# Down and output projections as one row on the tensor engine, output written as four rows

## The chip, the cores and the metric

The kernel runs on one core of a Trainium2 chip. The metric is device time in microseconds (us), the median of several executions. A profile gives the span of one execution, from its first to its last instruction; it is a little shorter than the time (2518.0 against 2519.67 for the profiled execution of the kernel before). A transfer has landed when the last of its DMA engines has raised its semaphore (a counter); the trace holds the time of every such count, called the records of the semaphores below. PE is the tensor engine, PEld its weight loads, DVE the vector engine, ACT the scalar engine, SP the engine that issues most DMAs.

## The reference, cut to what matters

One decode step: attention of one query over a cache of 65536 keys in 32 heads, a small gated feed-forward layer, and a gated sum of both.

```python
g = sigmoid((x * gate_w).sum(-1, keepdims=True))
# a: q = x @ wq; per head softmax(q k^T / sqrt(128)) v; heads joined (4096) @ wo   -> 512 numbers
# b: (silu(x @ w_gate) * (x @ w_up)) @ w_down                                      -> 512 numbers
return g * a + (1 - g) * b                                                      # bf16, (1, 1, 512)
```

The two caches are 1 GB together and are read once. Everything the change touches computes or stores the 512 output numbers.

Of the kernel before, what the change touches and what calls it, by code (L numbers as in the profile page):

```python
# [7 lines left out]
ACT = mybir.ActivationFunctionType  # L8
ALU = mybir.AluOpType
AXIS = mybir.AxisListType  # L10
P = 128
# [68 lines left out]
def kernel(  # L80
# [14 lines left out]
    nc = tc.nc  # L95
    bf16 = mybir.dt.bfloat16
    f32 = mybir.dt.float32

    _, H, Sk, Dh = A_k_cache.shape
    D = A_x.shape[2]  # L100
    F = B_w_gate.shape[1]
    KT = D // P
    FT = F // P
    OT = D // P
# [4 lines left out]
    scale = float(Dh) ** -0.5  # L109
# [7 lines left out]
    def sb(name, shape, dtype):  # L117
        return consts.tile(shape, dtype, name=name)
# [18 lines left out]
    O_sb = sb("O_sb", [VB, VB * Dh], f32)  # L137
    o_all = sb("o_all", [P, H], f32)
    oT = sb("oT", [P, H], bf16)
    gval = sb("gval", [P, 1], f32)  # L140
    ngval = sb("ngval", [P, 1], f32)
    hT = sb("hT", [P, FT], bf16)
# [2 lines left out]
    xg = sb("xg", [1, D], bf16)  # L145
    s_t = sb("s_t", [1, 1], f32)
    tot = sb("tot", [P, H], f32)
    rest = sb("rest", [P, OT], f32)
    o_row = sb("o_row", [H, Dh], bf16)
    M = sb("M", [P, H], bf16)  # L150
    o_last = sb("o_last", [P, 1], bf16)
    out_sb = sb("out_sb", [P, OT], bf16)

    S_ps = [psum.tile([P, HK, R], f32, name=f"S_ps{i}") for i in range(2)]
    O_ps = psum.tile([VB, VB * Dh], f32, name="O_ps")
    m_sp = psum.tile([P, 512], f32, name="m_sp")
    m_c = psum.tile([P, 512], f32, name="m_c")
    m_x = psum.tile([P, 512], f32, name="m_x")
# [7 lines left out]
    def op(engine, key, fn, reads=(), writes=(), sem=None):  # L166
        plan.add(engine, key, fn, list(reads), list(writes), sem)

    def units(s, a, b):

        w = UNIT * Dh
        return [(s, u) for u in range(a // w, -(-b // w))]

    def view(s, a, t, n):
        return slot[s][:, a : a + t * n].rearrange("p (t n) -> p t n", t=t)

    def dma(key, out_ap, in_ap, writes=(), reads=(), sem=None, engine="SP"):
        op(
            engine, key, lambda: emit[engine].dma_start(out=out_ap, in_=in_ap),
            reads=reads, writes=writes, sem=sem or key,  # L180
        )
# [11 lines left out]
    def take():  # L193
        s = turn[0] % SLOTS
        turn[0] += 1
        return s
# [27 lines left out]
    op("POOL", "ones_b", lambda: nc.gpsimd.memset(ones_b, 1.0), writes=["ones_b"])  # L224
    op("DVE", "ones", lambda: nc.vector.memset(ones, 1.0), writes=["ones"])
    op("DVE", "oT0", lambda: nc.vector.memset(oT, 0.0), writes=["oT"])
    op("DVE", "rowsum0", lambda: nc.vector.memset(rowsum, 0.0), writes=["rowsum"])

    def select(name, out_ap, in_ap, src, pattern, mul):
# [16 lines left out]
    def mms(key, out_ap, pairs, reads, writes, start=True, stop=True):  # L246


        def fn():
            for i, (a, b) in enumerate(pairs):  # L250
                ins = nc.tensor.matmul(  # L251
                    out_ap, lhsT=a, rhs=b,
                    start=start and i == 0, stop=stop and i == len(pairs) - 1,
                )
            return ins

        op("PE", key, fn, reads, writes)

    def group(key, parts, reads, writes):


        def fn():
            for out_ap, pairs in parts:
                for i, (a, b) in enumerate(pairs):
                    ins = nc.tensor.matmul(  # L265
                        out_ap, lhsT=a, rhs=b, start=(i == 0), stop=(i == len(pairs) - 1)
                    )
            return ins

        op("PE", key, fn, reads, writes)  # L270

    def act(key, out_ap, in_ap, func, reads, writes, **kw):
        op(
            "ACT", key, lambda: nc.scalar.activation(out=out_ap, in_=in_ap, func=func, **kw),  # L274
            reads, writes,
        )

    def dve(key, fn, reads, writes):
        op("DVE", key, fn, reads, writes)
# [36 lines left out]
    def block(n, j, m):  # L316

        s, h = where["k", n], n // CH
        qb = q_bc[h % 2]
        q_rep = bass.AP(tensor=qb.tensor, offset=qb.offset, ap=[list(qb.ap[0]), [0, m], [1, Dh]])  # L320
        w = view(s, 0, KPP, Dh)[:, j : j + m, :]
        names = units(s, j * Dh, (j + m) * Dh)
        dve(
            "products", lambda: nc.vector.tensor_tensor(out=w, in0=w, in1=q_rep, op=ALU.mult),  # L324
            names + [("q_bc", h % 2)], names,
        )
        r = ring["S"] % 2
        ring["S"] += 1
        B = 512 // R
        group(  # L330
            ("sums", s, j, m, r),
            [
                (
                    S_ps[r][:, b : b + B, :],
                    [(ident, w[:, b : b + B, i * R : (i + 1) * R]) for i in range(Dh // R)],
                )
                for b in range(0, m, B)
            ],
            names + ["ident"], [("S_ps", r)],
        )  # L340
        todo.append((n, j, m, r))

    def gather():
        n, j, m, r = todo.pop(0)
        b = ring["Sb"] % 2
        ring["Sb"] += 1
        dve(
            "gather",
            lambda: nc.vector.tensor_reduce(  # L349
                out=S_sb[b][:, :m], in_=S_ps[r][:, :m, :], axis=AXIS.X, op=ALU.add  # L350
            ),
            [("S_ps", r)], [("S_sb", b)],
        )
        col = n * RS + j // EK
        act(
            "exp", P_sb[n % 2][:, j : j + m], S_sb[b][:, :m], ACT.Exp,
            [("S_sb", b), "rowsum"], [("P_sb", n % 2, u) for u in range(j // EK, (j + m) // EK)]
            + [("rowsum", col)],
            scale=scale, accum_out=rowsum[:, col : col + 1],
        )  # L360
# [25 lines left out]
    def diagonal():  # L386

        h = pending.pop(0)
        mms(
            ("diagonal", h == H - 1), m_c[:, 0:1],  # L390
            [(O_sb[:, j * Dh : (j + 1) * Dh], pick[:, j : j + 1]) for j in range(VB)],
            ["O_sb", "pick"], ["m_c"], stop=(h < H - 1),
        )
        if h < H - 1:
            act("o_all", o_all[:, h : h + 1], m_c[:, 0:1], ACT.Copy, ["m_c"], [("o_all", h)])
# [45 lines left out]
            ["gval"], ["ngval"],  # L441
        )

    def rows(key, w_v, names, cols, cname, ks):

        group(
            key,
            [
                (
                    m_x[:, b : b + 1],  # L450
                    [(w_v[:, k, bass.ds(b, P, OT)], cols[:, k : k + 1]) for k in ks],
                )
                for b in range(OT)
            ],
            names + [cname], ["m_x"],
        )

    def norm(h0, h1):
        w = CH * RS
# [24 lines left out]
    def turn_outputs(part):  # L484

        if part == 0:
            mms("t_ps", m_sp[:H, :Dh], [(oT, ident)], ["oT", "ident"], ["m_sp"])
            act("o_row", o_row, m_sp[:H, :Dh], ACT.Copy, ["m_sp"], ["o_row"])
        else:
            mms(  # L490
                "m_ps", m_sp[:, :H],
                [(sel[:, j, :], o_row[:, j * H : (j + 1) * H]) for j in range(RP)],
                ["sel", "o_row"], ["m_sp"],
            )
            act("M", M, m_sp[:, :H], ACT.Copy, ["m_sp"], ["M"])
# [5 lines left out]
    for n in range(N - 1):  # L501
        h, c = divmod(n, CH)
# [27 lines left out]
    n, h = N - 1, H - 1  # L530
    ws = take()
    WO = FT * D
    WL = WO + H * D
    wd, wo, wo_last = view(ws, 0, FT, D), view(ws, WO, H, D), view(ws, WL, 1, D)
# [3 lines left out]
    load("k", n, [EK] * (KPP // EK))  # L538
    load("v", n, V_END)
    turn_outputs(1)  # L540
    rows("b_ps", wd, units(ws, 0, WO), hT, "hT", range(FT))
    diagonal()
    for i, j in enumerate(range(0, KPP, EK)):
        block(n, j, EK)
        if i == 0:
            dve("rest", lambda: nc.vector.tensor_scalar_mul(rest, m_x[:, :OT], ngval),
                ["m_x", "ngval"], ["rest"])
            rows("a_ps", wo, units(ws, WO, WL), M, "M", range(H))
        if i == 2:
            dve(  # L550
                "rest2",
                lambda: nc.vector.scalar_tensor_tensor(
                    out=rest, in0=m_x[:, :OT], scalar=gval, in1=rest, op0=ALU.mult, op1=ALU.add
                ),
                ["m_x", "gval", "rest"], ["rest"],
            )
        while len(todo) > 1:
            gather()
    gather()
# [3 lines left out]
    for m in V_END:  # L563
# [7 lines left out]
        if at == 0:  # L571
            norm(h, H)
        at += m
    dve("o_last", lambda: nc.vector.tensor_scalar_mul(o_last, m_c[:, 0:1], tot[:, h:H]),
        ["m_c", ("tot", h)], ["o_last"])
    rows("l_ps", wo_last, units(ws, WL, WL + D), o_last, "o_last", [0])
    dve(
        "out_sb",
        lambda: nc.vector.scalar_tensor_tensor(
            out=out_sb, in0=m_x[:, :OT], scalar=gval, in1=rest, op0=ALU.mult, op1=ALU.add  # L580
        ),
        ["m_x", "gval", "rest"], ["out_sb"],
    )
    dma("out", out[0, 0].rearrange("(p b) -> p b", b=OT), out_sb, ["out"], ["out_sb"])
    op("SP", "end", None, reads=["out"])


# [74 lines left out]
```

## The kernel before: the parts that the change touches

The caches stream in blocks of 8 MB through three slots. Per block of K, DVE multiplies by the query in place, PE sums the products (the tiles `S_ps`), DVE gathers, ACT takes the exponential, and PE multiplies by V. The last block of keys is handled apart, in four pieces ("the tail" below, some 40 us). Into its PE work the two projections are mixed, in *column* form: every 128x128 block of a weight matrix is the stationary operand, and one column of 128 numbers moves. A result lies as 128 partitions x 4.

```python
def rows(key, w_v, names, cols, cname, ks):
    group(key,
        [(m_x[:, b : b + 1],
          [(w_v[:, k, bass.ds(b, P, OT)], cols[:, k : k + 1]) for k in ks])   # every 4th weight column
         for b in range(OT)],                                                 # OT = 4
        names + [cname], ["m_x"])
# ... the tail, in program order (PE keeps this order):
rows("b_ps", wd, ..., hT, "hT", range(FT))            # down projection, 4 x 14 matmuls
diagonal()
for i, j in enumerate(range(0, KPP, EK)):             # four pieces of the last K block
    block(n, j, EK)                                   # DVE products, PE sums
    if i == 0:
        # rest = (1 - g) * b
        rows("a_ps", wo, ..., M, "M", range(H))       # output projection of 31 heads, 4 x 32 matmuls
    if i == 2:
        # rest = g * a + rest
    while len(todo) > 1:
        gather()                                      # DVE gather, ACT exp, one piece behind
gather()
# last head: five groups of one-column matmuls into m_c, 128 + 64 + 32 + 16 + 16,
# each waiting for its piece of the last V block; the softmax sum after the first
# o_last = m_c / sum;  rows("l_ps", wo_last, ..., o_last, "o_last", [0]);  out_sb = g * m_x + rest
dma("out", out[0, 0].rearrange("(p b) -> p b", b=OT), out_sb, ...)   # 128 pieces of 8 bytes
```

The softmax here doesn't subtract the row's maximum and nothing guards it: scores larger than these inputs give would overflow.

## Time and profile before

Before the change: 2522.19 us median of 3 runs (2521.62 to 2523.8).

| what | before |
|---|---|
| span of the profiled execution | 2518.0 us |
| DMA, one queue | 99.8% of the span |
| PE / DVE / ACT busy | 78% / 50% / 4% |
| down projection, output projection on PE | 2.03 us, 4.41 us |
| output DMA, issue to landing | 2.9 us |

From the page of the kernel before (span; busy us, share and instructions of the engines; the main DMA queue with packets, MB and share; bytes read):

```profile
span 2518.0 us, 19423 instructions
...
PE 1975.5 (78%) x9115; PEld 821.6 (33%) x9115; DVE 1268.3 (50%) x290; ACT 98.0 (4%) x402; POOL 1.9 (0%) x9
...
q1 hardware_dynamic: 20880, 1087.78, 99.8%
...
HBM read 1087.77 MB, written 0.00 MB: 432 GB/s over the span
...
```

The loads set the time of everything up to the tail. The timeline of the tail (start, duration, engine, source line, operation, output<-inputs, shapes, count, idle time before and who ended it):

```profile
...
2479.12 2.03 PE L265 MATMUL m_x<-hT,slot_66 128*128 128x1 bf16 x56
...
2485.91 4.41 PE L265 MATMUL m_x<-M,slot_66 128*128 128x1 bf16 x128
...
2490.18 5.30 PE L265 MATMUL S_ps_102<-slot_67,ident 128*128 128x512 bf16 x16
...
2500.59 3.63 PE L265 MATMUL S_ps_102<-slot_67,ident 128*128 128x512 bf16 x16 [1.66 <-DVE slot_67 L324]
...
2504.06 3.35 PE L251 MATMUL m_c<-P_sb_84,slot_65 128*128 128x1 bf16 x128
...
2511.11 1.74 PE L251 MATMUL m_c<-P_sb_84,slot_65 128*128 128x1 bf16 x60 [1.23 <-issue]
...
2512.88 0.22 DVE L574 TENSOR_SCALAR o_last<-m_c,tot 128x1 bf16<-128x1 f32 x1 [4.85 <-PE m_c L251]
...
2513.55 0.22 DVE L579 SCALAR_TENSOR_TENSOR out_sb<-m_x,gval,rest 128x4 bf16<-128x4 f32 x1 [0.45 <-PE m_x L265]
2513.80 0.35 SPq L179 DMA_DIRECT2D out_dram<-out_sb  x1
```

First come the two projections (56 and 128 matmuls of one column into `m_x`), with score sums (`S_ps`) behind them, then a wait of 1.66 us for DVE, the last sums, and the last head (`m_c`), which follows the pieces of V as they land. The chain of work that ended last, in order of time:

```profile
...
2479.87 29.69 DMA slot_65<-in_A_v_cache_dram
...
2509.61 0.27 PE m_c L251 x4
2509.88 1.23 issue
2511.11 1.75 PE m_c L251 x60
...
```

The chain runs through a landing of V and then through PE, with 1.23 us in which PE did nothing that the profile can explain. The records of the semaphores put the landing of the last V piece at 2512.07 us, so the last 16 matmuls could not have started before that. The DMA view gives the output transfer (last column: us from issue to landing):

```profile
...
out_dram<-out_sb SPq DMA_DIRECT2D x1, 1.0 KB, 2.9
```

One view more matters: the granted clock of PE (the share of its full clock that it was given). Length of a stretch, busy time of PE, PEld, DVE, ACT, POOL in it, then the mean clock, the DMA share and GB/s:

```profile
...
2486.00:2490.00 4.00, 4.00 (x124) 4.00 (x123) 4.00 (x3) 0.35 (x2) 0.00 (x0) 1.00 1.03 442
2490.00:2494.00 4.00, 4.00 (x21) 1.64 (x19) 2.32 (x2) 0.00 (x0) 0.00 (x0) 0.60 1.07 455
...
```

Right behind the 128 one-column matmuls the clock fell to half (from 2490.82 to 2494.23 in the trace's record of the clock, hence the mean of 0.60), and 16 sums took 5.30 us instead of 3.63.

### The profile page before, as it was taken

What the parts mean: (1) busy time and instruction counts of PE and PEld (TensorE: products, weight loads), DVE (VectorE), ACT (ScalarE), POOL (GpSimd) and SP (SyncE); (2) the same over time, 40 slices, a digit from 0 to 9 for tenths busy, and PEclk for the clock granted to TensorE, in tenths of its full rate; (3) what the DMA queues carried; (4) which work ended last, traced back from release to release, by engine and by line L of the source; (5) the groups of instructions that cost most, each with busy time, mean ns of one, the idle gap of its engine ahead of it and who ended that gap; (6) DMA issues with size and microseconds to landing.
All of it is one profiled execution on the core that took longest, in us unless ns stands there. A gap on an engine that the chain in (4) does not pass through costs nothing.

```text
span 2518.0 us, 19423 instructions
## 1 busy us (share of the span) xinstructions
PE 1975.5 (78%) x9115; PEld 821.6 (33%) x9115; DVE 1268.3 (50%) x290; ACT 98.0 (4%) x402; POOL 1.9 (0%) x9
## 2 busy tenths in 40 slices
PE   4787877877778778778787787787877877878788
PEld 2233332333323333333333333333333332333334
DVE  3455364464553554645535546445455464464554
ACT  0000000000000000000000000000000000000000
POOL 0000000000000000000000000000000000000000
PEclk8888989989889889898898899898988989989898
DMA  9999999999999999999999999999999999999998
GB/s 423 431 432 432 434 434 437 433 433 433 433 436 434 435 433 436 434 433 433 434 435 436 433 433 433 434 434 434 435 434 436 433 433 433 433 435 436 435 433 369
DMA packets 20906, 1088.09 MB, mean 432 GB/s; under 512 B 2450, under 2 KB 2580, under 8 KB 2836
## 3 DMA queue, kind: packets, MB, share of 16 engines
q1 hardware_dynamic: 20880, 1087.78, 99.8%
q8 instruction: 16, 0.26, 0.0%
q14 instruction: 6, 0.05, 0.0%
q10 hardware_dynamic: 4, 0.00, 0.0%
HBM read 1087.77 MB, written 0.00 MB: 432 GB/s over the span
## 4 chain that ended last, share of the span: by engine, by line
DMA 46%; PE 39%; DVE 13%; ACT 1%; another core or an unknown queue 0%; issue 0%; SPq 0%; DVEq 0%
PE O_ps L251 18%; DMA slot_67<-in_A_k_cache_dram 16%; DMA slot_66<-in_A_k_cache_dram 15%; DMA slot_65<-in_A_k_cache_dram 14%; PE S_ps_101 L265 11%; PE S_ps_102 L265 9%; DVE slot_67 L324 4%; DVE slot_66 L324 4%; DVE slot_65 L324 3%; DVE S_sb_82 L349 2%; PE m_c L251 1%; DMA slot_65<-in_A_v_cache_dram 1%; ACT P_sb_83 L274 1%; PE m_x L265 0%
## 5 line engine op out<-in xcount | busy, mean ns | idle before, releaser
L265 PE MATMUL S_ps_101<-slot_65,ident 128*128 128x512 bf16 x672 | 196.5, 465 | 133.8 <-DVE slot_65 L324 133.8
L265 PE MATMUL S_ps_101<-slot_66,ident 128*128 128x512 bf16 x672 | 193.5, 459 | 133.5 <-DVE slot_66 L324 133.5
L265 PE MATMUL S_ps_101<-slot_67,ident 128*128 128x512 bf16 x704 | 195.2, 446 | 125.0 <-DVE slot_67 L324 125.0
L324 DVE TENSOR_TENSOR slot_67<-slot_67,q_bc_79 128x16384 bf16<-128x16384 bf16 (+1 forms) x28 | 208.2, 7469 | 144.0 <-DMA slot_67<-in_A_k_cache_dram 144.0
L349 DVE TENSOR_REDUCE S_sb_82<-S_ps_102 128x128 f32<-128x1024 f32 (+1 forms) x67 | 78.8, 1176 | 391.5 <-PE S_ps_102 L265 391.5
L324 DVE TENSOR_TENSOR slot_65<-slot_65,q_bc_78 128x16384 bf16<-128x16384 bf16 x22 | 190.2, 8688 | 148.1 <-DMA slot_65<-in_A_k_cache_dram 148.1
L324 DVE TENSOR_TENSOR slot_66<-slot_66,q_bc_78 128x16384 bf16<-128x16384 bf16 (+1 forms) x24 | 190.6, 7977 | 136.5 <-DMA slot_66<-in_A_k_cache_dram 120.9
L324 DVE TENSOR_TENSOR slot_66<-slot_66,q_bc_79 128x16384 bf16<-128x16384 bf16 x20 | 172.9, 8688 | 123.9 <-DMA slot_66<-in_A_k_cache_dram 123.9
L324 DVE TENSOR_TENSOR slot_65<-slot_65,q_bc_79 128x16384 bf16<-128x16384 bf16 x20 | 172.9, 8688 | 118.5 <-DMA slot_65<-in_A_k_cache_dram 118.5
L324 DVE TENSOR_TENSOR slot_67<-slot_67,q_bc_78 128x16384 bf16<-128x16384 bf16 x20 | 172.9, 8688 | 117.5 <-DMA slot_67<-in_A_k_cache_dram 117.5
L251 PE MATMUL O_ps<-slot_67,P_sb_83 128*4 128x512 bf16 x704 | 156.4, 383 | 28.8 <-ACT P_sb_83 L274 18.3
L251 PE MATMUL O_ps<-slot_65,P_sb_83 128*4 128x512 bf16 x704 | 153.7, 379 | 19.6 <-ACT P_sb_83 L274 19.6
L251 PE MATMUL O_ps<-slot_66,P_sb_84 128*4 128x512 bf16 x704 | 153.7, 379 | 19.3 <-ACT P_sb_84 L274 19.3
L265 PE MATMUL S_ps_102<-slot_67,ident 128*128 128x512 bf16 x704 | 157.7, 382 | 3.1 <-DVE slot_67 L324 3.0
L265 PEld LDWEIGHTS S_ps_101<-slot_65,ident 128*128 128x128 bf16 x672 | 75.9, 116 | 254.6 <-DVE slot_65 L324 144.4
L265 PEld LDWEIGHTS S_ps_101<-slot_66,ident 128*128 128x128 bf16 x672 | 75.0, 115 | 252.0 <-DVE slot_66 L324 144.3
L265 PEld LDWEIGHTS S_ps_101<-slot_67,ident 128*128 128x128 bf16 x704 | 76.8, 112 | 243.1 <-DVE slot_67 L324 136.1
L251 PE MATMUL O_ps<-slot_67,P_sb_84 128*4 128x512 bf16 x640 | 139.7, 379 | 18.3 <-ACT P_sb_84 L274 18.3
L251 PE MATMUL O_ps<-slot_65,P_sb_84 128*4 128x512 bf16 x640 | 139.7, 379 | 18.3 <-ACT P_sb_84 L274 18.3
L251 PE MATMUL O_ps<-slot_66,P_sb_83 128*4 128x512 bf16 x640 | 139.7, 379 | 17.5 <-ACT P_sb_83 L274 17.5
L265 PE MATMUL S_ps_102<-slot_66,ident 128*128 128x512 bf16 x672 | 148.8, 379 | 2.1 <-DVE slot_66 L324 2.1
L265 PE MATMUL S_ps_102<-slot_65,ident 128*128 128x512 bf16 x672 | 148.6, 379 | 0.2 <-DVE slot_65 L324 0.2
(83 smaller groups left out, 860.6 us busy)
## 6 DMA issues: line engine op xcount, KB each, us to landing
slot_66<-in_A_k_cache_dram SPq DMA_DIRECT2D x4, 2048.0 KB, 24.6
slot_67<-in_A_k_cache_dram SPq DMA_DIRECT2D x4, 2048.0 KB, 30.6
slot_65<-in_A_wq_dram SPq DMA_DIRECT2D x1, 4096.0 KB, 12.2
slot_66<-in_A_wo_dram SPq DMA_DIRECT2D x1, 4096.0 KB, 31.3
slot_65<-in_A_v_cache_dram SPq DMA_DIRECT2D x1, 4096.0 KB, 23.2
slot_65<-in_A_v_cache_dram SPq DMA_DIRECT2D x1, 2048.0 KB, 27.7
slot_65<-in_B_w_gate_dram SPq DMA_DIRECT2D x1, 1792.0 KB, 34.9
slot_65<-in_B_w_up_dram SPq DMA_DIRECT2D x1, 1792.0 KB, 38.6
```

The source lines that it names most:

```text
L251: ins = nc.tensor.matmul(out_ap, lhsT=a, rhs=b, start=start and i == 0, stop=stop and i == len(pairs) - 1,)
L265: ins = nc.tensor.matmul(out_ap, lhsT=a, rhs=b, start=(i == 0), stop=(i == len(pairs) - 1))
L274: "ACT", key, lambda: nc.scalar.activation(out=out_ap, in_=in_ap, func=func, **kw),
L324: "products", lambda: nc.vector.tensor_tensor(out=w, in0=w, in1=q_rep, op=ALU.mult),
L349: lambda: nc.vector.tensor_reduce(out=S_sb[b][:, :m], in_=S_ps[r][:, :m, :], axis=AXIS.X, op=ALU.add),
```

## The change

The intent: fewer, longer matmuls for the projections (the vector is the stationary operand with one column, 512 weights move), and an output that leaves in 4 pieces of 256 bytes instead of 128 of 8. The row lies on one partition, so eight float32 matmuls with one-row operands spread it over four partitions; the last head is added there with four-column weights `Z` that are zero except in one column.

```diff
-    rows("b_ps", wd, units(ws, 0, WO), hT, "hT", range(FT))
+    row("b_ps", wd, units(ws, 0, WO), hT, "hT", range(FT), m_x, "m_x")      # 14 matmuls of 512
+    act("row_b", row_b, m_x[0:1, :D], ACT.Copy, ..., scale=ngval[0:1, :])
     diagonal()
     for i, j in enumerate(range(0, KPP, EK)):
         block(n, j, EK)
         if i == 0:
-            rest = m_x * ngval                                  # DVE
-            rows("a_ps", wo, units(ws, WO, WL), M, "M", range(H))
+            row("a_ps", wo, units(ws, WO, WL), M, "M", range(H), m_sp, "m_sp")  # 32 of 512
+            act("row_a", row_a, m_sp[0:1, :D], ACT.Copy, ..., scale=gval[0:1, :])
         if i == 2:
-            rest = m_x * gval + rest                            # DVE
+            mms("rest_ps", m_sp[:OT, :P],
+                [(unit[:, OT * q : OT * (q + 1)], r[:, P * q : P * (q + 1)])
+                 for r in (row_b, row_a) for q in range(OT)], ...)
+            act("rest", rest, m_sp[:OT, :P], ACT.Copy, ...)
@@ ... the last head is summed into m_c as before
-    o_last = m_c * tot;  rows("l_ps", wo_last, ..., o_last, "o_last", [0])
+    Z[:, :: OT + 1] = m_c * tot                                 # 128 x 4, into a zeroed 128 x 16
+    mms("l_ps", m_x[:OT, :P],
+        [(Z[:, OT * q : OT * (q + 1)], wo_last[:, 0, P * q : P * (q + 1)]) for q in range(OT)], ...)
     out_sb = m_x * gval + rest
-    dma("out", out[0, 0].rearrange("(p b) -> p b", b=OT), out_sb, ...)
+    dma("out", out[0, 0].rearrange("(i p) -> i p", p=P), out_sb, ...)
```

(Cut: three memsets at the start, and the declarations. The assignments without a call stand for one instruction each.)

More of the change, by code (lines that the diff above doesn't have):

```diff
@@ L147 @@
     tot = sb("tot", [P, H], f32)
-    rest = sb("rest", [P, OT], f32)
+    row_a = O_sb[0:1, :D]
+    row_b = sb("row_b", [1, D], f32)
+    unit = sb("unit", [1, OT * OT], f32)
+    rest = sb("rest", [OT, P], f32)
+    Z = sb("Z", [P, OT * OT], bf16)
     o_row = sb("o_row", [H, Dh], bf16)
     M = sb("M", [P, H], bf16)
-    o_last = sb("o_last", [P, 1], bf16)
-    out_sb = sb("out_sb", [P, OT], bf16)
+    out_sb = sb("out_sb", [OT, P], bf16)
     S_ps = [psum.tile([P, HK, R], f32, name=f"S_ps{i}") for i in range(2)]
@@ L226 @@
     op("DVE", "oT0", lambda: nc.vector.memset(oT, 0.0), writes=["oT"])
+    op("DVE", "Z0", lambda: nc.vector.memset(Z, 0.0), writes=["Z"])
+    op("DVE", "unit0", lambda: nc.vector.memset(unit, 0.0), writes=["unit"])
+    op("DVE", "unit1", lambda: nc.vector.memset(unit[:, :: OT + 1], 1.0), writes=["unit"])
     op("DVE", "rowsum0", lambda: nc.vector.memset(rowsum, 0.0), writes=["rowsum"])
@@ L442, in gate, with row @@
         )
-    def rows(key, w_v, names, cols, cname, ks):
-        group(
-            key,
-            [
-                (
-                    m_x[:, b : b + 1],
-                    [(w_v[:, k, bass.ds(b, P, OT)], cols[:, k : k + 1]) for k in ks],
-                )
-                for b in range(OT)
-            ],
-            names + [cname], ["m_x"],
-        )
+    def row(key, w_v, names, cols, cname, ks, bank, bname):
+        mms(key, bank[0:1, :D], [(cols[:, k : k + 1], w_v[:, k, :]) for k in ks],
+            names + [cname], [bname])
     def norm(h0, h1):
@@ L540 @@
     turn_outputs(1)
-    rows("b_ps", wd, units(ws, 0, WO), hT, "hT", range(FT))
+    row("b_ps", wd, units(ws, 0, WO), hT, "hT", range(FT), m_x, "m_x")
+    act("row_b", row_b, m_x[0:1, :D], ACT.Copy, ["m_x", "ngval"], ["row_b"], scale=ngval[0:1, :])
     diagonal()
@@ L545 @@
         if i == 0:
-            dve("rest", lambda: nc.vector.tensor_scalar_mul(rest, m_x[:, :OT], ngval),
-                ["m_x", "ngval"], ["rest"])
-            rows("a_ps", wo, units(ws, WO, WL), M, "M", range(H))
+            row("a_ps", wo, units(ws, WO, WL), M, "M", range(H), m_sp, "m_sp")
+            act("row_a", row_a, m_sp[0:1, :D], ACT.Copy, ["m_sp", "gval"], ["O_sb"],
+                scale=gval[0:1, :])
         if i == 2:
-            dve(
-                "rest2",
-                lambda: nc.vector.scalar_tensor_tensor(
-                    out=rest, in0=m_x[:, :OT], scalar=gval, in1=rest, op0=ALU.mult, op1=ALU.add
-                ),
-                ["m_x", "gval", "rest"], ["rest"],
+            mms(
+                "rest_ps", m_sp[:OT, :P],
+                [
+                    (unit[:, OT * q : OT * (q + 1)], r[:, P * q : P * (q + 1)])
+                    for r in (row_b, row_a)
+                    for q in range(OT)
+                ],
+                ["unit", "O_sb", "row_b"], ["m_sp"],
             )
+            act("rest", rest, m_sp[:OT, :P], ACT.Copy, ["m_sp"], ["rest"])
         while len(todo) > 1:
@@ L573 @@
         at += m
-    dve("o_last", lambda: nc.vector.tensor_scalar_mul(o_last, m_c[:, 0:1], tot[:, h:H]),
-        ["m_c", ("tot", h)], ["o_last"])
-    rows("l_ps", wo_last, units(ws, WL, WL + D), o_last, "o_last", [0])
+    dve(
+        "Z",
+        lambda: nc.vector.tensor_scalar_mul(
+            Z[:, :: OT + 1], m_c[:, 0:1].to_broadcast([P, OT]), tot[:, h:H]
+        ),
+        ["m_c", ("tot", h)], ["Z"],
+    )
+    mms(
+        "l_ps", m_x[:OT, :P],
+        [(Z[:, OT * q : OT * (q + 1)], wo_last[:, 0, P * q : P * (q + 1)]) for q in range(OT)],
+        ["Z"] + units(ws, WL, WL + D), ["m_x"],
+    )
     dve(
@@ L579 @@
         lambda: nc.vector.scalar_tensor_tensor(
-            out=out_sb, in0=m_x[:, :OT], scalar=gval, in1=rest, op0=ALU.mult, op1=ALU.add
+            out=out_sb, in0=m_x[:OT, :P], scalar=gval[:OT, :], in1=rest,
+            op0=ALU.mult, op1=ALU.add,
         ),
@@ L583 @@
     )
-    dma("out", out[0, 0].rearrange("(p b) -> p b", b=OT), out_sb, ["out"], ["out_sb"])
+    dma("out", out[0, 0].rearrange("(i p) -> i p", p=P), out_sb, ["out"], ["out_sb"])
     op("SP", "end", None, reads=["out"])
```

## The prediction

> **What bounds the kernel.** The page shows the DMA queue busy for 99.8% of the span, 1088 MB at 432 GB/s; PE is busy 78%, DVE 50%, ACT 4%. The loads of the K and V caches set the time. The change touches neither them nor anything in the loop (three small memsets at the start fall into idle DVE time), so all of its effect lies in the last 40 us of 2518.
>
> **The tail before (timeline and chain of waits, last 80 us).** The chain ends: V landing, `m_c` matmuls (to 2512.86), `o_last` 0.22, four `m_x` matmuls 0.28, `out_sb` 0.22, output DMA issued at 2513.80, landed about 2.9 us later, span end 2518.0. The landings put the last V piece at 2512.07, so the end is set by DMA, but PE runs close behind: its order is down projection (56 one-column matmuls, 2.03 us), diagonal 1.05, score sums 3.63, output projection (128 one-column matmuls, 4.41), sums 5.30, sums 3.6, a wait of 1.66 for DVE, sums 3.63, then `m_c`.
>
> **Costs on PE.**
> - Down projection: 14 matmuls of 512 columns, at the 227 ns a piece of the sums (3.63 us for 16): 3.2 us, +1.1; 0.3 us of it hides in an existing wait.
> - Output projection: 32 such, 7.2 us, +2.8.
> - The sums behind it ran at granted clock 0.5 from about 2490.9 to 2494 after the run of one-column matmuls, 5.30 us instead of 3.63. The Trainium skill, "TensorE: Matmul & The Clock Gate", Part 1, says that an idle window of about 3.4 us halves the clock[...]. 512-column matmuls should keep it at 1.0: -1.7.
> - New float32 spread, 8 matmuls recorded as 16 (the `pick` matmuls: 8 records in 1.05 us): estimate 2.2 us, of which 1.66 fits the wait for DVE: +0.5.
> Together the last sums end about 2.2 us later (estimate 1.5 to 4). `m_c` now starts at about 2506.3 instead of 2504; its 256 matmuls plus the norm need about 7.3 us: 2513.5 against 2512.86. A gap of 1.23 us before, at 2509.9, absorbs most of the delay. So about +0.5 us reaches the end (0 to 2).
>
> **The end.** `Z`, 4 matmuls with four-column weights, `out_sb`: each within 0.1 us of what it replaces. The output goes as 4 rows of 256 B instead of 128 pieces of 8 B. The old completions spread from 2515.1 to 2516.7; [...] 1.8 us passed between the last packet and the last completion. Only the spread can shrink: -0.3 to -1.5, say -0.8.
>
> **Sum.** +0.5 - 0.8: nothing visible. Predicted 2522 us (2517.5 to 2526.5, which is mainly variation between chips and runs). Faster by over 2%: 0.005; within 2%: 0.985; slower by over 2%: 0.01.
>
> **What would show it right or wrong.** Timeline of the tail: output projection 7 us, the sums after it 3.6 us, clock 1.0 in windows from 2490 to 2500 us; last sums ending 1.5 to 4 us later; `m_c` ending within 2 us of the last V landing, not limited by it alone; output landing under 2.9 us after issue. The first 2470 us identical, 432 GB/s.
>
> **What would make it wrong.** The clock dropping during the 512-column run (427 ns each would add some 7 us); float32 matmuls with a moving row of 128 much slower than estimated; an instruction fetch falling into the PE tail; the row copies on ACT (1 partition, 512 elements) delaying the exponentials; a different DMA rate on the chip used.

PE was busy for 4.00 us of the 4 from 2486 to 2490.

## The result, and the profile after

The changed kernel took 2519.97 us median of 4 runs (2519.86 to 2522.85), the kernel before 2521.9 in 4 runs (2520.1 to 2523.8). The ratio is 0.9995, interval 0.9978 to 1.0012: no difference can be seen. The page after:

```profile
span 2518.2 us, 19173 instructions
...
PE 1980.7 (79%) x8993; PEld 820.1 (33%) x8993; DVE 1268.7 (50%) x291; ACT 99.2 (4%) x405; POOL 1.9 (0%) x9
...
q1 hardware_dynamic: 20744, 1087.78, 99.7%
...
```

PE has 122 matmuls fewer and is busy 5 us longer; the loads moved the same bytes. The tail of the changed kernel, the same lines as before:

```profile
...
2480.20 3.18 PE L258 MATMUL m_x<-slot_66,hT 128*1 128x512 bf16 x14
...
2487.85 7.07 PE L258 MATMUL m_sp<-slot_66,M 128*1 128x512 bf16 x32
...
2494.85 3.63 PE L272 MATMUL S_ps_104<-slot_67,ident 128*128 128x512 bf16 x16
...
2503.70 3.63 PE L272 MATMUL S_ps_104<-slot_67,ident 128*128 128x512 bf16 x16
...
2507.16 3.40 PE L258 MATMUL m_c<-P_sb_84,slot_65 128*128 128x1 bf16 x128
...
2510.86 3.55 PE L258 MATMUL m_c<-P_sb_84,slot_65 128*128 128x1 bf16 x128
...
2514.45 0.23 DVE L580 TENSOR_SCALAR Z<-m_c,tot 128x4 bf16<-128x4 f32 x1 [3.04 <-PE m_c L258]
...
2515.36 0.34 DVE L592 SCALAR_TENSOR_TENSOR out_sb<-m_x,gval,rest 4x128 bf16<-4x128 f32 x1 [0.68 <-PE m_x L258]
2515.72 0.34 SPq L182 DMA_DIRECT2D out_dram<-out_sb  x1
```

The output projection takes 7.07 us instead of 4.41, but the sums behind it take 3.63 instead of 5.30, because the clock stays up:

```profile
...
2490.00:2494.00 4.00, 4.00 (x20) 1.60 (x19) 2.99 (x1) 0.00 (x0) 0.00 (x0) 1.00 1.04 442
...
```

From the start of the down projection to the end of the last sums, the changed kernel needs 2503.70 + 3.63 - 2480.20 = 27.13 us, the kernel before 2500.59 + 3.63 - 2479.12 = 25.10. PE reaches the last head later, and its chain shows no landing of V in this stretch:

```profile
...
2501.93 1.83 PE m_sp L258 x16
2503.77 3.56 PE S_ps_104 L272 x16
2507.33 3.24 PE m_c L258 x128
...
2511.01 3.42 PE m_c L258 x128
...
```

The last V piece landed at 2512.18 us, but PE did not finish `m_c` before 2514.41. So the end was set by PE, and the output DMA went out at 2515.72, 1.92 us later than before. It then landed at 2516.90, 1.18 us after issue, against 2.87 before (both from the records of the semaphore; the DMA view gives no landing for the new form). 1.92 lost and 1.69 won back leave the 0.2 us between the spans of 2518.2 and 2518.0.

One caution belongs here. The tail of this execution already *started* 1.08 us later than that of before (2480.20 against 2479.12). That is not the change: the first sums of the block before, the same instructions in both kernels, ran at half clock in this execution (5.33 us in the chain, from 2443.93) and at full clock in the other (3.63 us). That slow stretch comes and goes with either kernel: it is there in the kernel before with nine outputs (below), and absent in the second run of the changed kernel. Traces of these kernels start their tail anywhere between 2479.0 and 2483.0 us. Below, stretches are therefore counted from the start of the down projection.

### The profile page after: what moved, and what is told of

Same layout as the page of the kernel before. It is cut to its first block, busy times and chain, and to the rows that moved or that the text cites. A ratio compares the mean times of both kernels' runs of the same rounds, so it can differ in the third digit from the quotient of the medians.

```text
span 2518.2 us, 19173 instructions
## 1 busy us (share of the span) xinstructions
PE 1980.7 (79%) x8993; PEld 820.1 (33%) x8993; DVE 1268.7 (50%) x291; ACT 99.2 (4%) x405; POOL 1.9 (0%) x9
## 4 chain that ended last, share of the span: by engine, by line
DMA 44%; PE 41%; DVE 13%; ACT 1%; another core or an unknown queue 0%; issue 0%; SPq 0%; DVEq 0%; ACTq 0%
PE O_ps L258 18%; DMA slot_67<-in_A_k_cache_dram 16%; DMA slot_66<-in_A_k_cache_dram 14%; DMA slot_65<-in_A_k_cache_dram 14%; PE S_ps_103 L272 12%; PE S_ps_104 L272 9%; DVE slot_67 L331 4%; DVE slot_66 L331 4%; DVE slot_65 L331 3%; DVE S_sb_82 L356 2%; PE m_c L258 1%; ACT P_sb_83 L281 1%; DMA slot_65<-in_A_wq_dram 0%; PE m_sp L258 0%; PE m_x L272 0%
```

## The experiments

Theory: PE work in the tail reaches the end of the changed kernel, and costs about 2 us; the output transfer is about 1.7 us shorter, because its pieces are larger; the two cancel. Rivals: the end is set by the loads and neither matters; or the old landing was slow only because loads had just ended; or the number of DMA engines that report, not the size of the pieces, makes the old landing slow.

### The output transfer, nine times in a row

The first four kernels ran on one chip, one execution each. The addition is

```diff
     dma("out", ...)
+    for _ in range(8):
+        dma("out", ..., ["out"], ["out_sb"])      # each waits for the one before it
```

to the kernel before (128 pieces of 8 bytes) and to the changed kernel (4 of 256):

> The kernel before, its output DMA (128 pieces of 8 B) issued nine times in a row, each after the one before it has landed. Theory: landing took 2.87 us from issue in the profile of before and stands on the end of the span, so eight more add 8 x about 2.95, some 24 us: span near 2542. Rival (the long landing of before came from the loads still in flight just before it, not from its form): the eight repeats run on an idle memory and take 1.2 to 1.5 us each, 10 to 12 us in all.

> The changed kernel, its output DMA (4 rows of 256 B) nine times in a row. Theory: 1.18 us each as in the profile of after, with the issue about 1.25: eight more add about 10 us, span near 2528. Rival: the form does not matter, then the same addition as in the run with 128 pieces.

In the third kernel the four rows of the changed kernel are written in pieces of 8 bytes (`out[0, 0].rearrange("(r q b) -> q r b", q=OT, b=OT)`; the result is permuted, wrong), in the fourth a zeroed tile of 16 rows of 64 bytes is written (also wrong):

> The changed kernel with its four rows written in pieces of 8 B (result permuted, wrong on purpose), nine times. If the size of the pieces makes the landing slow, about 2.9 us each (+24 us); if the number of DMA engines that must report does (16 before, 4 after), about 1.2 us each (+10 us).

> The changed kernel, but the output written from a zeroed tile of 16 rows of 64 B (wrong on purpose), nine times. If the size or the number of the pieces makes the landing slow, 64 B pieces land nearly as the rows of 256 B do, 1.2 to 1.5 us each (+10 to 12 us); if the number of DMA engines does, about 2.9 us (+24 us).

The timelines (SPq: start of the first issue, time to the end of the last) in that order: 128 pieces of 8 bytes,

```profile
...
2514.56 28.08 SPq L179 DMA_DIRECT2D out_dram<-out_sb  x9
```

4 rows of 256 bytes,

```profile
...
2518.15 9.56 SPq L182 DMA_DIRECT2D out_dram<-out_sb  x9
```

4 rows in pieces of 8 bytes,

```profile
...
2515.93 29.64 SPq L182 DMA_DIRECT2D out_dram<-out_sb  x9
```

16 rows of 64 bytes,

```profile
...
2515.69 10.84 SPq L183 DMA_DIRECT2D out_dram<-fake  x9
```

(The spans were 2547.3, 2529.9, 2550.1 and 2528.8 us.) The stretch contains eight full transfers and one last issue of 0.35 us. One transfer took (28.08 - 0.35) / 8 = 3.47 us with 128 pieces of 8 bytes, (9.56 - 0.35) / 8 = 1.15 with 4 of 256, (29.64 - 0.35) / 8 = 3.66 with 8 bytes from four partitions, and (10.84 - 0.35) / 8 = 1.31 with 16 of 64. The loads were over, so "the loads disturbed it" falls; the theory's own 2.95 per transfer with 8-byte pieces was somewhat low. The Trainium skill, "DMA: Bandwidth & Descriptors", section "Why a DMA increments its semaphore by 16 and not by 1", says how many DMA engines take part: 16 for a tile of 128 or 16 rows, 4 for 4 rows, with the issuing sequencer adding the missing increments at once. The trace agrees: a transfer of the kernel before leaves 16 increments, one of the changed kernel five, the first 0.46 us after issue and the others at 1.12 to 1.18. Sixteen engines with 64 bytes are fast and four engines with 8 bytes are slow, so the number of engines is not the cause; the pieces are. Size and number of the pieces change together in these runs: in both fast forms each engine carries one piece, in the slow ones 8 and 32 (128 pieces over 16 and over 4 engines). Which of these it is stays open.

### Does the output form alone account for its share?

In the changed kernel only the output DMA is altered: it writes 128 pieces of 8 bytes from a zeroed tile, still waiting for the result. Its output is wrong, which doesn't matter for the time. Five rounds.

> The changed kernel with nothing altered but the output DMA: 128 pieces of 8 B from a zeroed tile, waiting for the same result (wrong on purpose). Theory: the output lands 2.5 to 3.3 us after issue instead of 1.2, span 1.3 to 2.1 us longer than the changed kernel, 2519.3 to 2520. Rival (the output form is hidden): 2518.

```profile
...
2516.30 0.35 SPq L183 DMA_DIRECT2D out_dram<-fake  x1
```

```profile
...
out_dram<-fake SPq DMA_DIRECT2D x1, 1.0 KB, 2.9
```

The first fence is the end of its timeline, the second its DMA view. From the start of the down projection (2480.79) to the output issue it needs 35.51 us, the changed kernel 2515.72 - 2480.20 = 35.52: nothing else changed. The landing went from 1.18 to 2.89 us. The span was 2520.5 us, a little over the range, since this execution's tail had also started 0.6 us later. The median was 2522.19 us (2521.39 to 2523.96), ratio to before 1.0006 (0.9992 to 1.0020). The rival, an output form that is hidden, falls.

### One half of the change at a time

These ran together with the changed kernel on one chip, five rounds each; the kernel before had 2521.39 us median there (9 runs, 2519.78 to 2523.92).

> The changed kernel once more, as the reference of this set. Theory: the end is set by PE, m_c ends 1 to 2.5 us after the last V landing, output lands about 1.2 us after issue, span 2516.5 to 2518.5, median within 1.5 us of before.

It took 2520.07 us (2519.6 to 2521.24), ratio 0.9995 (0.9982 to 1.0009), span 2517.9. `m_c` ended at 2514.09, 2.0 us after the last V landing (2512.06), and the output landed 1.18 us after issue. From the start of the down projection to the end of the last sums: 27.12 us, the 27.13 of the first trace.

First the projections as rows, but turned back to 128x4 columns, with last head and output as before:

```diff
-    rows("b_ps", ...);  rows("a_ps", ...)
+    row("b_ps", ..., m_x, "m_x");  row("a_ps", ..., m_sp, "m_sp")     # as in the changed kernel
+    # at i == 2: m_sp[:, b] = sum over r of (row_b, row_a) of r[:, b::4] (weights) x [[1.0]]
     dma("out", out[0, 0].rearrange("(p b) -> p b", b=OT), out_sb, ...)
```

> Only the first half of the change: both projections as one row on PE, but then spread to 128x4 columns, last head and output DMA as before. Theory (PE work added in the tail reaches the end, and the output form pays it back): last sums end as late as after (about 27 us from the start of the down projection, against 25.1 before), output landing 2.9 us, span 1.5 to 2 us longer than after, about 2519.5. Rival (PE has slack in the tail and the end is set by the loads): m_c ends as before, span 2518.0.

It took 2524.83 us (2523.44 to 2525.76), ratio 1.0010 (0.9997 to 1.0024), with a span of 2524.0: 4.5 us worse than expected. The timeline:

```profile
...
2503.12 0.62 PE L267 MATMUL m_sp<-ones,row_b 1*128 1x1 f32 x2
...
2506.97 5.00 PE L267 MATMUL S_ps<-slot,ident 128*128 128x512 bf16 x16
...
```

This way of turning the row back was a bad tool. Eight float32 matmuls with 128-column weights took from 2503.12 to 2506.97, 3.85 us instead of the 1.83 of the spread in the changed kernel. They move one column each; while they ran, at 2506.37, the clock fell to half, and the last sums took 5.00 us instead of 3.63. Another 1.3 us is chance: this tail started at 2481.46, that of the changed kernel at 2480.20. The three (2.0, 1.4 and 1.3) about make up the 4.5. The run agrees with the theory in sign (more PE work before the last sums ends later), but it does not isolate the rows; the single-change run above does that for the output side.

Then the other half. The projections are columns, with each weight block contiguous, the sum is turned to four rows by one matmul, and last head and output are those of the changed kernel:

```diff
-    row("b_ps", ...);  row("a_ps", ...);  spread by `unit`
+    rows(...) with w_v[:, k, P * b : P * (b + 1)] as weights       # 56 and 128 one-column matmuls
+    mms("rest_ps", m_sp[:OT, :P], [(rest_c, ident_f)], ...)         # 128x4 -> 4x128, float32
```

> Only the second half: both projections as columns as before, the sum turned to four rows by one matmul, last head and output DMA as after. Theory: last sums 25.1 to 26 us from the start of the down projection, clock at 0.5 for about 3.4 us after the output projection, m_c ends less than 1 us after the last V landing, output lands in 1.2 us: span about 2516.3, 1.5 us under both kernels. Rival (the output form is worth nothing by itself): span 2518.

It took 2518.27 us in five runs (2518.27 to 2518.35), ratio 0.9986 (0.9973 to 1.0000), and is correct: the fastest kernel, and the steadiest. Its slowest run was faster than the fastest of the 9 runs of the kernel before (2519.78) and of the 5 of the changed kernel (2519.6) on this chip, so this gain of over 1 us shows in the times too. Timeline, then chain:

```profile
...
2486.08 3.35 PE L270 MATMUL m_x<-M,slot 128*128 128x1 bf16 x128
...
2514.09 0.35 SPq L181 DMA_DIRECT2D out_dram<-out_sb  x1
```

```profile
...
2481.86 30.27 DMA slot<-in_A_v_cache_dram
...
2512.18 0.60 PE m_c L256 x16
...
```

The chain (its DMA line ends at 2512.13) now goes straight from the landing of the last V piece to the last 16 matmuls and the end: PE had caught up and waited for every piece of V. The output landed at 2515.26, 1.17 us after issue; the span was 2516.6, 1.4 us under that of before and 1.6 under that of the changed kernel. Two lines of the expectation were missed: the clock stayed at 1.00 (mean of 2488 to 2492), and the last sums ended 2498.02 + 3.63 - 2480.15 = 21.50 us after the start of the down projection instead of 25.1 to 26. They would fit the 4.41 us of the strided weights.

This run differs from before in two things, the output form and the contiguous weights. So the second alone was put into the kernel before (result permuted, wrong), five rounds, on the chip of the run with only the output altered:

```diff
-    [(w_v[:, k, bass.ds(b, P, OT)], cols[:, k : k + 1]) for k in ks]
+    [(w_v[:, k, P * b : P * (b + 1)], cols[:, k : k + 1]) for k in ks]
```

> The kernel before with its column matmuls loading contiguous weight blocks instead of every fourth column (result permuted, wrong on purpose); this is the other thing in which the run with columns and a row output differs from before. Theory: the 128 projection matmuls take 3.35 us instead of 4.41 and the clock stays at 1.0 behind them, so PE reaches the last V pieces earlier and waits for them; the output still lands 2.9 us after issue: span 2517.5 to 2518, clearly over the 2516.6 of columns with row output. Rival (the faster columns were the gain, not the output): span about 2516.6.

```profile
...
2486.13 3.35 PE L265 MATMUL m_x<-M,slot 128*128 128x1 bf16 x128
...
2498.07 3.63 PE L265 MATMUL S_ps<-slot,ident 128*128 128x512 bf16 x16 [1.66 <-DVE slot L324]
...
2512.20 0.59 PE L251 MATMUL m_c<-P_sb,slot 128*128 128x1 bf16 x16 [0.60 <-DMA slot<-in_A_v_cache_dram]
...
2513.73 0.35 SPq L179 DMA_DIRECT2D out_dram<-out_sb  x1
```

```profile
...
out_dram<-out_sb SPq DMA_DIRECT2D x1, 1.0 KB, 3.0
```

128 matmuls took 3.35 us instead of 4.41. The tail to the end of the last sums shrank from 25.10 us to 2498.07 + 3.63 - 2480.18 = 21.52, and the last `m_c` group started at 2512.20, right after V landed at 2512.15. Nevertheless the span was 2518.0, exactly that of before in the first profile, and the median 2519.72 us (2519.32 to 2520.22), where the kernel before had 2520.38 (2519.54 to 2522.57) on this chip, ratio 0.9996 (0.9982 to 1.0009). So PE work was not what set the end of the kernel before. The tail had started 1.06 us later than that of before and ended with it; the times spread over 0.9 us in 5 runs, those of the kernel before over 3.0 in 9. Both suggest that the faster columns absorb a late start, but five runs do not show it. From here to columns with row output, the output is issued 2514.09 - 2513.73 = 0.36 us later and the landing is 2.99 - 1.17 = 1.82 us shorter: 1.46 us, the 1.4 of the spans. The gain was the output's.

### More work, or less, on PE in the tail

The output projection done twice, in each kernel (one execution each, the results are right):

> The changed kernel with the output projection's 32 row matmuls done twice (the second overwrites the first, the result is right). Theory: PE sets the end of the changed kernel, so all of the extra 7.1 us reaches it: m_c ends 7 us later, span about 2525. Rival (the loads set it): span under 2520.

> The kernel before with the output projection's 128 one-column matmuls done twice (result right). Theory: 4.4 us more on PE, less the slack of about 1.5 us that PE had before the last V landing: span 2 to 4 us longer, 2520.5 to 2522; the longer stretch of one-column matmuls lets the granted clock drop for more of the sums behind it, which could add 1.7 us. Rival (no slack): the full 4.4 us or more.

The changed kernel with 64 row matmuls:

```profile
...
2487.80 13.97 PE L258 MATMUL m_sp<-slot,M 128*1 128x512 bf16 x64
...
2520.95 0.23 DVE L581 TENSOR_SCALAR Z<-m_c,tot 128x4 bf16<-128x4 f32 x1 [2.95 <-PE m_c L258]
...
```

The 6.90 us added on PE (13.97 - 7.07) came out as a span of 2524.7 us against 2518.2, 6.5 more, with the same start of the tail (2480.15 and 2480.20). PE sets the end of the changed kernel (one execution, so its state is unknown).

The kernel before with twice the columns missed its range: span 2526.3, 8.3 us more than before. Its tail began 1.8 us later than that of before, by the half clock again; the first sums in the tail ran at half clock too (6.25 us), and the longer columns had a gap of 1.03 us within them. The run can't measure the slack of the kernel before, and is not used for it; the run with contiguous weights above shows that PE was not the limit there.

Last, the changed kernel without the spread: the row stays on one partition, one matmul of 512 columns adds the last head, and the output is one piece of 1 KB.

```diff
-    mms("rest_ps", ...unit...);  act("rest", ...)
+    row_b = m_sp[0:1, :D] * gval + row_b            # DVE, 1 x 512
-    dma("out", out[0, 0].rearrange("(i p) -> i p", p=P), out_sb, ...)
+    dma("out", out[0], out_sb, ...)
```

> As after, but without the spread: the row stays on one partition, last head added by one matmul of 512 columns, output one piece of 1 KB. Theory: PE saves the 1.83 us of the spread in front of the last sums, loses about 0.5 us at the end to a matmul and a DVE instruction of 512 elements: span about 1 us under after, 2516 to 2517. Rival (PE not on the critical path): 0.5 us longer than after.

```profile
...
2502.62 3.63 PE L265 MATMUL S_ps<-slot,ident 128*128 128x512 bf16 x16 [1.66 <-DVE slot L324]
...
2512.60 1.47 PE L251 MATMUL m_c<-P_sb,slot 128*128 128x1 bf16 x50 [0.95 <-issue]
...
2515.10 0.74 DVE L571 SCALAR_TENSOR_TENSOR out_sb<-m_x,gval,row_b 1x512 bf16<-1x512 f32 x1 [0.77 <-PE m_x L251]
...
```

It took 2520.14 us (2519.7 to 2521.65), ratio 0.9995, span 2518.3: nothing gained. That is the number of the rival (0.5 us over the 2517.9 of the second run of the changed kernel), but the doubled projection has shown that PE is on the path, so the rival's reason does not hold. The expectation was wrong in one step. Without the spread PE waits 1.66 us for DVE in its place, and the tail to the end of the last sums is 2502.62 + 3.63 - 2479.23 = 27.02 us, only 0.1 less than with it. PE had no idle time there in the changed kernel, so the chain of waits ran through the spread, but the next link, DVE's products of the fourth piece, ended at 2503.55, only 0.15 us before the last sums began at 2503.70. On the other side the end grew: the last DVE instruction takes 0.74 us for 1x512, where 4x128 take 0.34.

## Why the prediction was right, point by point

- "Predicted 2522 us (2517.5 to 2526.5)": 2519.97 measured, within the range, and no visible change. With 9 us of range and terms of 1 or 2 us, this tests little; the steps below do.
- Bound by the loads outside the tail: right; 432 GB/s and the same bytes.
- Down projection 3.2 us: 3.18. Output projection 7.2: 7.07. Clock at 1.0 behind it and 3.6 us for the sums: right, 1.00 and 3.63. The reason given, an idle window, did not fit: PE was busy when the clock fell in the kernel before.
- Last sums "about 2.2 us later": 2.03 from the start of the down projection. The estimate of the spread, 2.2 us, was 1.83 in the chain, nearly all in the wait for DVE, as the run without it shows; "+0.5" was about +0.1.
- "About +0.5 us reaches the end (0 to 2)": mis-sized. `m_c` ended 1.56 us later. This execution began its tail 1.08 us later for a reason that is not the change, and the prediction had no term for that. Counted from the start of the down projection, `m_c` ended 0.48 us later in the first trace after (34.20 against 33.72) and 1.35 later in the second (35.07). The gap of 1.23 us, which was to absorb the delay, is no fixed slack: it was absent in the first trace after, and there again, with 1.07 us, in the second. Pairs of traces with nearly the same start free the issue of the output from that chance: 2515.41 (second trace after, tail from 2479.02) against 2513.80 (before, 2479.12), and 2515.72 (first trace after, 2480.20) against 2514.56 (kernel before with nine outputs, 2480.43). So the change moved the issue by some 1.2 to 1.6 us (in the second pair, only the kernel before has the gap).
- "Only the spread can shrink: -0.3 to -1.5, say -0.8": the mechanism was right, the size was off. It measured -1.69. In the old transfer the first engine had reported 1.26 us after issue and the last 2.87; with four pieces the last reports at 1.18, so the whole spread went.
- The sum, "+0.5 - 0.8: nothing visible", held as +1.92 at the issue and -1.69 at the landing: two larger terms of opposite sign, the first partly chance (1.2 to 1.6 without it). That their errors cancelled was luck.

What is not shown: whether the medians, some 1 to 2 us apart, differ because of the change. The intervals of the ratios are 7 to 9 us wide.

## What to carry to other kernels

An output of a few hundred numbers that leaves as many pieces of 8 bytes ends a kernel late, here by 1.7 us in 2.9; turn it so that it leaves in a few pieces of 64 bytes or more, if the turn costs less than that on the critical path. Measure the path in the tail by taking work out or putting work in: a link in the chain of waits may have another one a tenth of a microsecond behind it, and then removing it gains nothing. With a vector times a matrix, long rows on PE were slower here than contiguous one-column matmuls (7.07 against 3.35 us).

## What the Trainium skill lacked or had wrong

- "DMA: Bandwidth & Descriptors", Specifications, warns of pieces under 512 B for line rate, but gives no landing time for a store in many small pieces: here 128 pieces of 8 B landed in 2.9 us alone and 3.47 us repeated, 16 of 64 B in 1.31 and 4 of 256 B in 1.15, all of them under 512 B.
- The same page, Anatomy of one DMA, fits about 2.0 us of fixed cost for the path of the GpSimd queue, and has no such fit for SP. A store of 1 KB issued by SP landed in 1.18 us here.
- "TensorE: Matmul & The Clock Gate", Part 1, gives a free-running window of 3413 ns and says that idleness halves the clock. It lacks that the clock can fall behind one-column matmuls while PE counts as 100% busy: in both traces with a stretch of 128 strided columns (4.4 us) it fell within 1 us after its end, for 3.41 us; in both where the output projection has contiguous ones (3.35 us) it stayed at 1.0. Contiguous ones are not safe for that: in all 14 traces the clock fell 2.4 to 5.4 us after the 256 contiguous one-column matmuls of the last head began, in the first trace after (2.41 us) without a pause of PE. What decides stays open.
- The same page, Weight-path perf modes, allows packed or strided reads for its fast weight load and gives no cost for the stride: a pair of weight load and one-column matmul took 4.41 / 128 = 34 ns with every fourth column and 3.35 / 128 = 26 ns with contiguous ones.
- "Runtime: NRT & Kernel Launch", Instruction fetch mechanics, says that instruction fetch is mostly hidden. In six of the traces PE stood still for 0.95 to 1.57 us inside a run of one-column matmuls, each time with a 16 KB read on the instruction queue of about 0.9 us that ended 1.3 to 1.5 us before PE went on. Traces of one kernel stop at the same instruction (after 196 of the 256 matmuls into `m_c` in two of the kernel before, after 191 in two of the changed kernel), but four other traces of the changed kernel do not stop there. That the fetch is the cause is argued, not shown.
